# The up-projection of a fused kernel's second block as seven block products in place of eight

## The chip, the cores and the metric

One NeuronCore of a Trainium2 chip runs the whole program. Its engines are TensorE (PE, matmul), whose weight loads are shown apart (PEld), VectorE (DVE), ScalarE (ACT), GpSimd (POOL) and SyncE (SP), which here only issues DMAs. The time is that of one execution on the device in microseconds; lower is better. The comparison is between the kernel before and the changed one.

## The reference

Three stages follow each other. Attention over 2 batches, 8 heads, 768 positions of 64, with a mask that lets a query see only keys of its own hash bucket. A gated block with a spatial projection over the 768 positions (width 512, inner width 1024). And the second block, which the change is about:

```python
mu = np.mean(x, axis=-1, keepdims=True)
var = np.mean((x - mu) ** 2, axis=-1, keepdims=True)
xn = (x - mu) / np.sqrt(var + 1e-06) * g_ln
ch = np.maximum(xn @ w_ch1, 0.0) @ w_ch2
return (x + ch).astype(np.float32)
```

Here x has 2 x 768 = 1536 rows of 512, `w_ch1` is 512 x 2048 and `w_ch2` 2048 x 512. The weights arrive as float64.

## The kernel before, in words

**Precision.** A matmul of the second block is done in three passes of float32r (`PASSES`): each operand is split into a high and a low part, and high x high, high x low and low x high are summed in PSUM (`mm3`). The high part is a copy (`split_hi_v` on ScalarE), the low part a subtraction (`split_lo` on GpSimd, `split_lo_v` on VectorE).

**Weights.** A piece of a weight matrix, 128 x 512 values, is loaded as raw 64-bit words by a DMA that ScalarE issues (`stage_f64`). `words_f64` turns it into two float32 words: one absolute value on ScalarE, then five VectorE operations (clamp, shift and mask, two-operand bit operation, mask, two-operand product). `join_f64` adds the two words on GpSimd, and `split_f64` makes the high part on ScalarE and the low part on GpSimd. In the trace these are `f_w` (the staged words), `f64c_w` (the working tile), `w1t` and `w2t` (the parts). Staging and working tiles have two buffers each (`CB = 2`).

**The second block.** The 2048 inner columns are 16 tiles `f` of 128. The 1536 rows are three chunks `c` of 512 (`TCH`). `up(c, f)` makes one tile of the inner activations transposed, `pc` (128 x 512), with 4 x 3 matmuls of 512 columns; ScalarE writes the relu as high part of `ch`, VectorE the low part, `max(pc, 0) - high`, which reads `pc` in PSUM. `down(c, f)` multiplies `ch`, as the stationary operand, with `w2t[f]` into four accumulators `acc` (one for 128 rows), 4 x 3 matmuls of 512 columns. Not all weights fit, so `runs` visits the chunks in seven runs over ranges of `f`; at the end of a run the accumulators are added to the tiles `ot`, which hold the residual (`residual` loads them from `y_dram`). `second(n)` puts the `up` of one step ahead of the `down` of the step before. The layer norm of a chunk is `ln_stats` (statistics, then `xc`) and `ln_x` (transposes `px_c`, split into `xh`).

**Parts and order.** The program has three parts: the attention with the first gated block of batch 0; part 1, the gated block of batch 1 (`moe1`), with the first steps of the second block as filling (`fill`); and part 2, the rest of the second block. Every engine does all its instructions of a part ahead of those of the next. Inside a part a planner (`Plan`) sets the order: `add` records every operation as a job (up to `RUN` matmuls of one target make one), `run` plays the jobs through with costs of its own, and `issue` writes them out in the order found. An engine other than TensorE may take a job only when TensorE has come within `LOOK` jobs of it (`opened`), and, unless the job is marked `soon`, not more than `EARLY` = 20 us ahead of the latest time (`latest`) at which it is due. All instructions are issued from one line, so every row of the trace has L498; they are told apart by the tiles that they write and read.

## Time and profile before

| | us |
|---|---|
| median of 3 runs (660.79 to 663.34) | 661.33 |
| the profiled execution | 661.69 |
| its span, first to last instruction | 659.6 |

| engine | busy us | share of the span | instructions |
|---|---|---|---|
| PE | 648.2 | 98% | 3386 |
| PEld | 506.7 | 77% | 3386 |
| DVE | 430.1 | 65% | 805 |
| ACT | 302.8 | 46% | 584 |
| POOL | 194.9 | 30% | 185 |

A row of a list of groups reads: line, engine, operation, what it writes <- what it reads, shapes, x count, then busy us, mean ns of one, and the idle time of the engine before them with what ended it. Matmuls are pipelined: the length of one is longer than the distance to the next, and the distance is what it costs.

### The profile page before, as it was taken

What the parts mean: (1) busy time and instruction counts of PE and PEld (TensorE: products, weight loads), DVE (VectorE), ACT (ScalarE), POOL (GpSimd) and SP (SyncE); (2) the same over time, 40 slices, a digit from 0 to 9 for tenths busy, and PEclk for the clock granted to TensorE, in tenths of its full rate; (3) what the DMA queues carried; (4) which work ended last, traced back from release to release, by engine and by line L of the source; (5) the groups of instructions that cost most, each with busy time, mean ns of one, the idle gap of its engine ahead of it and who ended that gap; (6) DMA issues with size and microseconds to landing.
All of it is one profiled execution on the core that took longest, in us unless ns stands there. A gap on an engine that the chain in (4) does not pass through costs nothing.

```text
span 659.6 us, 9420 instructions
## 1 busy us (share of the span) xinstructions
PE 648.2 (98%) x3386; PEld 506.7 (77%) x3386; DVE 430.1 (65%) x805; ACT 302.8 (46%) x584; POOL 194.9 (30%) x185
## 2 busy tenths in 40 slices
PE   7999999999999999999999999999999999999997
PEld 5676667767787787877788888788888888888886
DVE  6879779697886554543897995799862466612122
ACT  6788776876666455433564352533321222311110
POOL 3233424234555311200343331144440134510000
PEclk9999999999999999999999999999999999999999
DMA  6776876668644742606353530733310122200031
GB/s 155 198 196 151 276 168 177 171 145 287 183 114 128 223 104 77 210 16 242 118 210 118 164 93 33 270 97 95 96 34 32 65 64 68 92 1 17 0 112 64
DMA packets 48157, 83.51 MB, mean 127 GB/s; under 512 B 5792, under 2 KB 32112, under 8 KB 47344
## 3 DMA queue, kind: packets, MB, share of 16 engines
q1 hardware_dynamic: 33888, 53.42, 28.6%
q10 hardware_dynamic: 14224, 29.50, 13.7%
q8 instruction: 27, 0.44, 0.3%
q14 instruction: 18, 0.15, 0.1%
HBM read 51.52 MB, written 12.58 MB: 97 GB/s over the span
## 4 chain that ended last, share of the span: by engine, by line
PE 90%; DVE 4%; DMA 2%; ACT 2%; SPq 1%; issue 1%; POOL 0%; DVEq 0%; ACTq 0%
PE pc L498 20%; PE acc L498 20%; PE pv L498 10%; PE po L498 9%; PE sc L498 8%; PE pg L498 8%; PE pt L498 8%; PE py L498 5%; DMA qs<-m 2%; DVE x L498 1%; ACT x L498 1%; PE px_c L498 1%; PE ptr_g L498 1%; SPq L498 1%; DVE f64c_u L498 1%
## 5 line engine op out<-in xcount | busy, mean ns | idle before, releaser
L498 PE MATMUL pc<-xh,w1t 128*128 128x512 f32 x576 | 142.0, 394 | 0.0
L498 PE MATMUL acc<-w2t,ch 128*128 128x512 f32 x576 | 141.8, 393 | 0.0
L498 PEld LDWEIGHTS acc<-w2t,ch 128*128 128x128 f32 x576 | 108.1, 188 | 24.8 <-DVE ot L498 0.2
L498 PEld LDWEIGHTS pc<-xh,w1t 128*128 128x128 f32 x576 | 107.8, 188 | 24.5
L498 ACT ACTIVATE x<-x,nb 128x768 f32<-128x768 f32 x96 | 89.7, 935 | 32.0 <-DVE x L498 30.0
L498 DVE SCALAR_TENSOR_TENSOR ch<-pc,ch 128x512 fp32r<-128x512 f32 x48 | 32.9, 686 | 101.6 <-ACT ch L498 101.6
L498 DVE TENSOR_SCALAR_CACHE_REDUCE x<-sc 128x768 f32<-128x768 f32 x96 | 91.0, 952 | 10.1 <-PE sc L498 3.8
L498 PE MATMUL sc<-ks,qs 128*128 128x512 f32 (+3 forms) x384 | 92.8, 362 | 4.6 <-DMA qs<-m 2.2
L498 ACT ACTIVATE ch<-pc 128x512 fp32r<-128x512 f32 x48 | 28.7, 598 | 130.6 <-PE pc L498 130.1
L498 POOL TENSOR_TENSOR f64c_w<-f_w,f64c_w 128x512 f32<-128x512 f32 x32 | 45.0, 1407 | 133.4 <-DVE f64c_w L498 115.7
L498 PE MATMUL pt<-ident,x 128*128 128x128 f32 x576 | 81.0, 274 | 1.0 <-ACT x L498 0.8
L498 PEld LDWEIGHTS sc<-ks,qs 128*128 128x128 f32 (+1 forms) x384 | 64.1, 190 | 18.9 <-issue 3.6
L498 PEld LDWEIGHTS pt<-ident,x 128*128 128x128 f32 x576 | 66.3, 141 | 13.2 <-issue 4.9
L498 ACT ACTIVATE e<-pt 128x384 f32<-128x384 f32 x120 | 55.3, 485 | 25.3 <-PE pt L498 25.1
L498 PE MATMUL po<-e,vv 128*64 128x384 f32 x384 | 65.5, 490 | 0.0
L498 DVE COPY e<-pt 128x384 f32<-128x384 f32 x72 | 39.6, 552 | 22.3 <-PE pt L498 22.2
L498 PEld LDWEIGHTS po<-e,vv 128*64 128x64 f32 x384 | 26.1, 137 | 31.2 <-issue 29.8
L498 DVE TENSOR_SCALAR f64c_w<-f64c_w 128x512 f32<-128x512 f32 (+1 forms) x64 | 37.3, 587 | 14.1 <-ACT f64c_w L498 13.1
L498 PE MATMUL pg<-vn,w_sp 128*128 128x512 f32 x180 | 43.9, 396 | 0.0
L498 PEld LDWEIGHTS pg<-vn,w_sp 128*128 128x128 f32 x180 | 33.1, 188 | 6.8
L498 ACT ACTIVATE f64c_w<-f_w 128x512 f32<-128x512 f32 x32 | 21.2, 668 | 34.7 <-DMA f_w<-in_w 33.5
L498 PE MATMUL py<-w_out,act_g 128*128 128x512 f32 x144 | 36.0, 396 | 0.0
(131 smaller groups left out, 787.1 us busy)
## 6 DMA issues: line engine op xcount, KB each, us to landing
f_w<-in_w ACTq DMA_DIRECT2D x32, 512.0 KB
ks<-k SPq DMA_DIRECT2D x45, 192.0 KB
qs<-q SPq DMA_DIRECT2D x30, 192.0 KB
wst_sp<-in_w_spT SPq DMA_DIRECT2D x12, 384.0 KB
w_out<-ws_out SPq DMA_DIRECT2D x2, 2048.0 KB
vv<-in_v SPq DMA_DIRECT2D x16, 192.0 KB
ot<-y_dram SPq DMA_DIRECT2D x12, 256.0 KB
qs<-q SPq DMA_DIRECT2D x30, 96.0 KB
```

Of the source, the lines that this page charges most:

```text
L498: getattr(getattr(nc, engine[j.engine]), op)(*map(live, args), **{k: live(x) for k, x in kw.items()})
```

## The change

The rows are cut into four chunks of 384 (`TCH = S // 2`), so that a batch is two chunks. The first four inner tiles (`NA`) are done as before, with matmuls of 384 columns. The other twelve are taken in six pairs `r`. For a pair and a batch the product of a 2 x 2 block matrix of weights (two inner tiles by two halves of the 512 inputs) with a 2 x 2 block matrix of inputs (two halves of the inputs by two chunks) is made from seven block products in place of eight, by sums of weights (`sums` in `w1_pair`, four on VectorE), differences of inputs (`x_forms`) and sums of products (`products`: two copies on ScalarE, five adds on VectorE and two on GpSimd). A pair and a batch are called a unit; there are twelve, in the order (1,2), (0,2), (0,3), (1,3), (1,4), ... The splits of a form into high and low part are made in `parts`. The relu of these tiles is taken from sums held in SBUF (`held`), not from PSUM. Both PSUM banks of the up-projection are taken in turn (`bank`).

The down-projection of a unit (`share`, 2 chunks x 3 row tiles x 2 inner tiles x 3 passes) is issued between the products of the following unit (`late`). Six accumulators are open at once. At the end of a run of units the accumulators are added to their rows, which are read from `y_dram` and written back (`gather_load`, `gather_tile`), the last time into the output. The conversion of the next pair's weights (`convert`) is issued between the products. In the planner `LOOK` is 50 jobs, twice that in part 2, and due times are counted from the first. Conversions in part 2 are marked `soon`.

The chunks' layer norm and the first steps move with the new chunks: in part 1 eight pieces of weights in place of ten, the statistics of three chunks, and the plain steps of chunk 0 and half of chunk 1. The list `fill` of part 1 is left out below, and so are the pools.

```diff
     RUN = 6
-    LOOK = 60
+    LOOK = 50
     EARLY = 20.0
     BULK = 14.0
...
-            i = bisect_left(reached, j.at - self.LOOK)
+            i = bisect_left(reached, j.at - (2 * self.LOOK if j.part > 1 else self.LOOK))
...
-        return late
+        first = min(late.values())
+        return {j: t - first for j, t in late.items()}
...
-    TCH = 512
+    TCH = S // 2
...
-    NA = 5
-    NW = 11
+    NA = 4
+    OB = 2
+    UB = 6
+    NP2 = NF2 // 2
...
+        if f % 2 == 0:
+            pool = m2 if f >= NA and f // 2 % 2 == 0 else m2a
+            w2t[f // 2] = pool.tile([P, 2, 2, DM], F32R, tag="wd", name=f"w2_{f}", bufs=1 if f >= NA and f // 2 % 2 == 0 else 2)
+        to = w2t[f // 2][:, f % 2]
+        if f < NA:
+            load_f64(to[:, 0:1], to[:, 1:2], w2[:, f : f + 1, :], f"w2_{f}")
+        else:
+            tf = join_f64(*words_f64(stage_f64(w2[:, f : f + 1, :], f"w2_{f}"), f"w2_{f}"))
+            hi_a(to[:, 0:1], tf)
+            split_lo(to[:, 1:2], tf, to[:, 0:1])
...
+    def w1_pair(r):
+
+        pool, n = (m2, 7) if r % 2 == 0 else (m2a, 8)
+        two = {}
+
+        def words(a):
+            if a == 0:
+                w1q[r] = pool.tile([P, 2, n, 2, P], F32R, tag="wf", name=f"w1_{r}", bufs=1)
+            f = 2 * r + a
+            nm = f"w1_{f}"
+            st = stage_f64(w1[:, :, f * P : (f + 1) * P], nm)
+            two[a] = join_f64(*words_f64(st, nm))
+            two["st", a] = st
+
+        def sums():
+            s = [two["st", 1][:, m].bitcast(F32).rearrange("p (k m) t -> p k (m t)", k=2) for m in range(4)]
+            two["s"] = s
+            a11, a12, a21, a22 = (two[a][:, 2 * k : 2 * k + 2] for a in range(2) for k in range(2))
+            nc.vector.tensor_tensor(s[0], a21, a22, op=ALU.add)
+            nc.vector.tensor_tensor(s[1], s[0], a11, op=ALU.subtract)
+            nc.vector.tensor_tensor(s[2], a11, a21, op=ALU.subtract)
+            nc.vector.tensor_tensor(s[3], a12, s[1], op=ALU.subtract)
+
+        def parts():
+            q = w1q[r]
+            raw = two[0].rearrange("p (h k) n -> p h k n", h=2)
+            for at, src in (
+                (slice(0, 2), raw),
+                *((3 + m, two["s"][m]) for m in (1, 0, 2)),
+                (2, two[1][:, 2:4]),
+                (6, two["s"][3]),
+            ):
+                hi_a(q[:, 0, at], src)
+                split_lo(q[:, 1, at], src, q[:, 0, at])
+
+        return [lambda: words(0), lambda: words(1), sums, parts]
...
+    def bank(name):
+        turn[0] += 1
+        return ps_c.tile([P, 512], F32, tag=f"p{turn[0] % 2}", name=name, bufs=1)
...
+    def quarter(c, f):
+        chs[c, f] = m2a.tile([P, 2, TCH], F32R, tag="ch", name=f"ch_{c}_{f}", bufs=6)
+        return chs[c, f]
+
+    def relu_split(ch, src):
+        nc.scalar.activation(ch[:, 0], src, AF.Relu)
+        nc.vector.scalar_tensor_tensor(ch[:, 1], src, 0.0, ch[:, 0].bitcast(F32), op0=ALU.max, op1=ALU.subtract)
...
-        pc = ps_c.tile([P, 512], F32, tag="pc", name=f"pc_{c}_{f}")
-        mm3(pc, [(lambda i, k=k: w1t[f][:, i, k, :], lambda j, k=k: xhs[c][:, j, k, :]) for k in range(KFT)])
-        ch = m2a.tile([P, 2, TCH], F32R, tag="ch", name=f"ch_{c}_{f}", bufs=2)
-        nc.scalar.activation(ch[:, 0], pc, AF.Relu)
-        nc.vector.scalar_tensor_tensor(ch[:, 1], pc, 0.0, ch[:, 0].bitcast(F32), op0=ALU.max, op1=ALU.subtract)
-        chs[c, f] = ch
+        pc = bank(f"pc_{c}_{f}")[:, :TCH]
+        w = w1q["A"][:, f]
+        mm3(pc, [(lambda i, k=k: w[:, i, k, :], lambda j, k=k: xhs[c][:, j, k, :]) for k in range(KFT)])
+        relu_split(quarter(c, f), pc)
...
+    def x_forms(b):
+
+        h0, h1 = xhs[2 * b], xhs[2 * b + 1]
+        t = {}
+        for n in (3, 1, 2, 4):
+            for a in range(2):
+                if b:
+                    t[n, a] = m2.tile([P, 2, TCH], F32R, name=f"t{n}{a}_{b}", bufs=1)
+                elif n == 1:
+                    t[n, a] = h1[:, a, 0:2]
+                else:
+                    t[n, a] = m2a.tile([P, 2, TCH], F32R, tag="xc", name=f"t{n}{a}_{b}", bufs=6)
+        if not b:
+            for c, h in enumerate((h0, h1)):
+                rxs[c] = m2.tile([P, KFT, TCH], F32, tag=f"rx{c}", name=f"rx_{c}", bufs=1)
+                for k in (0, 2):
+                    nc.gpsimd.tensor_tensor(
+                        rxs[c][:, k : k + 2],
+                        h[:, 0, k : k + 2].bitcast(F32),
+                        h[:, 1, k : k + 2].bitcast(F32),
+                        op=ALU.add,
+                    )
+        r11, r21, r12, r22 = (rxs[2 * b + c][:, k : k + 2] for c in range(2) for k in (0, 2))
+        for n, to, x, y in ((1, r11, r12, r11), (3, r12, r22, r12), (2, r22, r22, r11), (4, r21, r21, r22)):
+            nc.vector.tensor_tensor(to, x, y, op=ALU.subtract)
+            hi_a(t[n, 0], to)
+            (split_lo_v if n % 2 else split_lo)(t[n, 1], to, t[n, 0])
+        forms[b] = {
+            "B11": lambda j, k: h0[:, j, k],
+            "B21": lambda j, k: h0[:, j, 2 + k],
+            "B22": lambda j, k: h1[:, j, 2 + k],
+            **{f"T{n}": lambda j, k, n=n: t[n, j][:, k] for n in (1, 2, 3, 4)},
+        }
...
+    def products(b, r):
+
+        f0, f1, c0, c1 = 2 * r, 2 * r + 1, 2 * b, 2 * b + 1
+        q, rhs = w1q[r], forms[b]
+        nm = f"{b}_{r}"
+
+        def product(n, a, x):
+            ps = bank(f"p{n}_{nm}")[:, :TCH]
+            for m, (k, (i, j)) in enumerate((k, ij) for k in range(2) for ij in PASSES):
+                nc.tensor.matmul(ps, q[:, i, a, k], rhs[x](j, k), start=(m == 0), stop=(m == 5))
+            return ps
+
+        def held(n):
+            return m2.tile([P, TCH], F32, tag="u", name=f"u{n}_{nm}", bufs=UB)
+
+        def plus(to, x, y, e=nc.vector):
+            e.tensor_tensor(to, x, y, op=ALU.add)
+
+        u, c = held(1), held(2)
+        nc.scalar.activation(u, product(1, 0, "B11"), AF.Copy)
+        yield
+        plus(c, product(2, 1, "B21"), u)
+        relu_split(quarter(c0, f0), c)
+        yield
+        plus(u, product(6, 4, "T2"), u)
+        yield
+        w, v = held(5), held(7)
+        nc.scalar.activation(w, product(5, 3, "T1"), AF.Copy)
+        yield
+        plus(v, product(7, 5, "T3"), u)
+        plus(u, u, w, nc.gpsimd)
+        plus(w, w, v, nc.gpsimd)
+        yield
+        x = held(4)
+        plus(x, product(4, 2, "T4"), v)
+        relu_split(quarter(c0, f1), x)
+        yield
+        relu_split(quarter(c1, f1), w)
+        plus(u, product(3, 6, "B22"), u)
+        relu_split(quarter(c1, f0), u)
+        yield
...
+    def share(c, t, fs, start, stop):
+
         if start:
-            accs[c] = [ps_y.tile([P, 512], F32, tag="py", name=f"acc_{c}_{f}_{t}") for t in range(TPC)]
-        for t in range(TPC):
+            at = c % 2 * TPC + t
+            pool, tag = (ps_n, "m") if c > 1 and at > 3 or c < 2 and plan.part == 2 and at > 3 else (ps_y, "py")
+            accs[c, t] = pool.tile([P, 512], F32, tag=tag, name=f"acc_{c}_{fs[0]}_{t}")
+        for f in fs:
+            ch = chs[c, f]
             for n, (i, j) in enumerate(PASSES):
                 nc.tensor.matmul(
-                    accs[c][t],
+                    accs[c, t],
                     ch[:, i, t * P : (t + 1) * P],
-                    w2t[f][:, j, 0, :],
-                    start=(start and n == 0),
-                    stop=(stop and n == 2),
+                    w2t[f // 2][:, f % 2, j],
+                    start=(start and f == fs[0] and n == 0),
+                    stop=(stop and f == fs[-1] and n == 2),
...
+    def gather_load(c, last=False):
+        if last and c > 1:
+            if c == 3:
+                ots["last"] = m2a.tile([P, 2, TPC, DM], F32, tag="xh0", name="ots_last", bufs=1)
+            ots[c] = ots["last"][:, c - 2]
+        else:
+            ots[c] = m2.tile([P, TPC, DM], F32, tag=f"rx{c % 2}", name=f"ots_{c}", bufs=1)
+        nc.sync.dma_start(out=ots[c], in_=y_dram[c * TPC : (c + 1) * TPC].rearrange("t p d -> p t d"))
+
+    def gather_tile(c, t, last=False, end=False):
+        n = c * TPC + t
+        ot = ots[c][:, t]
+        to = outv[n] if last else y_dram[n]
+        for a, cols in enumerate([slice(k * DM // 2, (k + 1) * DM // 2) for k in range(2)] if end else [slice(0, DM)]):
+            nc.vector.tensor_tensor(ot[:, cols], accs[c, t][:, cols], ot[:, cols], op=ALU.add)
+            (nc.scalar if a else nc.sync).dma_start(out=to[:, cols], in_=ot[:, cols])
...
-    runs = [(0, 0, NA), (1, 0, NA), (2, 0, NW), (1, NA, NW), (0, NA, NF2), (1, NW, NF2), (2, NW, NF2)]
-    cf = [(c, f, f == at, f == to - 1) for c, at, to in runs for f in range(at, to)]
-    todo = []
-
-    def second(n):
-        if n < len(cf):
-            up(*cf[n][:2])
-        if 1 <= n <= len(cf):
-            down(*cf[n - 1])
+    ps_c = Pool(plan, "ps_c", 1, part=1, after=(ps_s, ps_b), space=PSUM, reuse_waits="tile")
+    ps_y = Pool(plan, "ps_y", 4, part=1, after=(ps_b,), space=PSUM, reuse_waits="tile")
+
+    def plain(c, f):
+
+        if f < NA:
+            up(c, f)
+        if f:
+            down(c, f - 1, f == 1, f == NA and c < 2)
...
+    todo = []
+
+    def convert(r):
+        todo.extend(w1_pair(r))
+        todo.extend([lambda: w2_piece(2 * r), lambda: w2_piece(2 * r + 1)])
+
+    def next_todo():
+        plan.soon = True
+        if todo:
+            todo.pop(0)()
+        plan.soon = False
+
+    convert(NA // 2)
+    for f in range(NA + 1):
+        plain(2, f)
+        next_todo()
+        if f == 0:
+            for t in range(TPC):
+                ln_x(3, t)
+    for f in range(NA + 1):
+        plain(3, f)
+        if f < NA:
+            next_todo()
+        if f == 0:
+            x_forms(1)
+    while todo:
+        next_todo()
+    units = []
+    for r in range(NA // 2, NP2):
+        units.extend([(1, r), (0, r)] if r % 2 == 0 else [(0, r), (1, r)])
+    runs = []
+    for b, r in units:
+        if runs and runs[-1][0] == b:
+            runs[-1][1].append(r)
+        else:
+            runs.append((b, [r]))
+    late = []
+    for n, (b, rs_of) in enumerate(runs):
+        for m, r in enumerate(rs_of):
+            u = units.index((b, r))
+            if n == 0:
+                convert(r + 1)
+            elif m == len(rs_of) - 1 and r + 1 < NP2:
+                convert(r + 1)
+            if u == 0:
+                x_forms(0)
+            for _ in products(b, r):
+                if late:
+                    late.pop(0)()
+                next_todo()
+            while late:
+                late.pop(0)()
+            first, end = n > 0 and m == 0, m == len(rs_of) - 1
+            last = r == NP2 - 1
+
+            final = last and n == len(runs) - 1
+
+            def piece(c, t, fs, r=r, first=first, end=end, last=last, final=final):
+                share(c, t, fs, first and fs[0] == 2 * r, end and fs[-1] == 2 * r + 1)
+                if end and fs[-1] == 2 * r + 1:
+                    if t == 0:
+                        gather_load(c, last)
+                    gather_tile(c, t, last, final and c % 2 == 0 and t == TPC - 1)
+
+            both = (2 * r, 2 * r + 1)
+            for c, fs in ((2 * b, both[:1]), (2 * b + 1, both), (2 * b, both[1:])) if final else ((2 * b + 1, both), (2 * b, both)):
+                late.extend(lambda c=c, t=t, fs=fs, p=piece: p(c, t, fs) for t in range(TPC))
...
```

## Rows read from the trace of the kernel before

**Rows 1.** Page: busy us (share of the span) x instructions; granted clock in 40 slices.
```profile
PE 648.2 (98%) x3386; PEld 506.7 (77%) x3386; DVE 430.1 (65%) x805; ACT 302.8 (46%) x584; POOL 194.9 (30%) x185
...
PEclk9999999999999999999999999999999999999999
```

**Rows 2.** Waits of PE, longest first: us in total, times, longest.
```profile
PE sc L498 <- DMA qs<-m: 2.2, 2, 1.6
PE sc L498 <- DVE x L498: 1.6, 2, 0.9
...
```

**Rows 3.** Timeline of PE in the second block: start us, length us, what, count.
```profile
597.48 2.96 PE L498 MATMUL pc<-xh,w1t 128*128 128x512 f32 x12
...
603.03 2.96 PE L498 MATMUL pc<-xh,w1t 128*128 128x512 f32 x12
```

**Rows 4.** Groups by form, whole span: matmuls of `pc`, weight loads of `acc`.
```profile
L498 PE MATMUL pc<-xh,w1t 128*128 128x512 f32 x576 | 142.0, 394 | 0.0
...
L498 PEld LDWEIGHTS acc<-w2t,ch 128*128 128x128 f32 x576 | 108.1, 188 | 24.8 <-DVE ot L498 0.2
```

**Rows 5.** Stretches: us, PE, PEld, DVE, ACT, POOL busy (x), clock, DMA share, GB/s.
```profile
340.00:360.00 20.00, 20.00 (x90) 16.34 (x89) 18.31 (x39) 9.20 (x15) 9.57 (x8) 1.00 0.39 125
...
440.00:460.00 20.00, 20.00 (x88) 16.29 (x87) 18.69 (x24) 6.21 (x10) 9.56 (x7) 1.00 0.33 97
...
480.00:500.00 20.00, 20.00 (x89) 16.30 (x88) 10.27 (x13) 4.17 (x7) 6.51 (x5) 1.00 0.10 28
```

**Rows 6.** Timeline of PE at one score tile: 512, 256, 256 columns, then transposes.
```profile
121.68 0.64 PE L498 MATMUL sc<-ks,qs 76*128 76x512 f32 x3
122.16 0.60 PE L498 MATMUL pt<-ident,x 128*128 128x128 f32 x4
```

**Rows 7.** Groups by form, whole span: prices of other engines' operations.
```profile
L498 POOL TENSOR_TENSOR w1t<-f64c_w,w1t 128x512 fp32r<-128x512 f32 x16 | 21.0, 1315 | 10.9 <-ACT w1t L498 8.9 <-issue 1.8 <-POOL r_c L498 0.2
...
L498 ACT ACTIVATE e<-pt 128x384 f32<-128x384 f32 x120 | 55.3, 485 | 25.3 <-PE pt L498 25.1
...
L498 DVE COPY e<-pt 128x384 f32<-128x384 f32 x72 | 39.6, 552 | 22.3 <-PE pt L498 22.2
...
L498 POOL TENSOR_TENSOR w_sp<-wst_sp,w_sp 128x768 fp32r<-128x768 f32 x6 | 11.1, 1853 | 39.2 <-PE pg L498 37.7 <-issue 1.6
...
L498 DVE TENSOR_TENSOR w_sp_early<-wst_sp,w_sp_early 128x768 fp32r<-128x768 f32 x2 | 1.9, 948 | 0.0
...
L498 DVE TENSOR_TENSOR ot<-acc,ot 128x256 f32<-128x256 f32 x2 | 0.8, 420 | 0.0
```

**Rows 8.** Tile `f64c_w`, 425 to 470 us: ns shortest/median/longest, first and last start.
```profile
L498 DVE TENSOR_SCALAR f64c_w<-f64c_w x16: 409/428/1555, 426.1 to 468.9; 128x512 f32<-128x512 f32 x8, 128x512 uint32<-128x512 uint32 x8
L498 DVE SCALAR_TENSOR_TENSOR f64c_w<-f_w,f64c_w x8: 676/681/693, 425.5 to 466.5; 128x512 f32<-128x512 uint32 x8
...
L498 DVE SCALAR_TENSOR_TENSOR f_w<-f_w,f64c_w x8: 675/693/1837, 428.5 to 469.3; 128x512 uint32<-128x512 uint32 x8
L498 DVE TENSOR_SCALAR f64c_w<-f_w x7: 426/1401/1414, 429.2 to 466.0; 128x512 uint32<-128x512 uint32 x7
```

**Rows 9.** Timeline of all engines from 431.9 us: GpSimd's join and VectorE beside it.
```profile
431.92 1.31 POOL L498 TENSOR_TENSOR f64c_w<-f_w,f64c_w 128x512 f32<-128x512 f32 x1 [1.56 <-DVE f64c_w L498]
432.16 1.82 DVE L498 TENSOR_SCALAR f64c_w<-f64c_w 128x512 f32<-128x512 f32 x2 [0.32 <-ACT f64c_w L498]
```

**Rows 10.** Tiles `ch`, `w_sp` and `k`: ns shortest/median/longest, first and last start.
```profile
L498 DVE SCALAR_TENSOR_TENSOR ch<-pc,ch x48: 655/691/695, 341.6 to 651.0; 128x512 fp32r<-128x512 f32 x48
...
L498 DVE TENSOR_TENSOR w_sp<-wst_sp,w_sp x4: 948/1590/2032, 355.6 to 392.6; 128x768 fp32r<-128x768 f32 x4
...
L498 POOL TENSOR_TENSOR k<-k x14: 1006/1013/1728, 24.4 to 222.3; 128x384 fp32r<-128x384 f32 x14
```

**Rows 11.** Timeline of ACT where part 2 begins: first weight loads, first word.
```profile
412.83 0.94 ACTq L498 DMA_DIRECT2D f_w<-in_w  x2
...
417.06 0.66 ACT L498 ACTIVATE f64c_w<-f_w 128x512 f32<-128x512 f32 x1 [0.79 <-DMA f_w<-in_w]
```

110 lines of the change are left out of this document (56 added, 54 removed).

## The prediction, made before the changed kernel was timed

> **What bounds the kernel now.** I read the page first: TensorE is busy 98% of the span at full clock, and no other engine comes near [rows 1]. A busy PE need not be a PE at its peak, so the waits come next: the two longest that the trace finds for TensorE, 2.2 and 1.6 us, belong to the scores `sc` of the attention, and nothing of the second block is in the list [rows 2]. The timeline of PE in the second block shows what its time is made of: twelve matmuls `pc` (up) and twelve `acc` (down) follow each other, and from one `pc` run to the next it takes 603.03 - 597.48 = 5.55 us, so 0.2312 us for each matmul of 512 columns [rows 3]. That is the price of the second block: 576 + 576 matmuls [rows 4] at 0.2312 = 266 of the 659.6 us. Fewer columns through TensorE is a gain one for one, as long as the other engines keep feeding it. How near these are to not doing so the table of stretches shows [rows 5]: VectorE is busy 18.3 and 18.7 of 20 us at 340 and 440, with GpSimd at 9.6 beside it, and TensorE never stops there; from 480 VectorE is down to 10, and the DMA engines to a tenth.
>
> **The change, part by part.**
>
> *Up-projection, removed and added.* Before: 16 inner tiles x 3 chunks x 12 matmuls = 576 of 512 columns, 576 x 0.2312 = 133.2 us. After: four tiles stay plain, 4 x 4 chunks x 12 = 192 matmuls of 384 columns; the other twelve are six pairs, each with 2 batches x 7 products x 6 matmuls, 504 of 384 columns. Together 696. The trace has no float32r matmul of 384 columns. The timeline of one score tile gives 256: from the start of the 76-row matmul of 512 columns to the next transpose it takes 122.16 - 121.68 = 0.48 us for one of 512 and two of 256 columns, so (0.48 - 0.231) / 2 = 0.1245 us each [rows 6]. Between that and 0.2312 lies 0.178; in proportion to the columns it would be 0.173. I take 0.175: 696 x 0.175 = 121.8 us, a gain of 11.4 us (9.3 at 0.178, 12.8 at 0.173).
>
> *Down-projection and transposes.* 16 tiles x 12 token tiles x 3 = 576 matmuls of 512 columns as before, and 48 transposes `px_c` as before: 0.
>
> *What the seven products ask of the others.* Prices: a VectorE operation of 384 columns 0.55 us (copies `e`), of 512 0.68, of 256 0.42, of 768 0.95; ScalarE at 384 0.485; GpSimd's two-operand operation 1.32 at 512, 1.01 at 384 (shortest and median), 1.85 at 768 [rows 7, 8, 10]. VectorE: 12 units x 5 adds x 0.55 = 33.0; six pairs x 4 weight sums x 0.42 = 10.1; input differences and their splits 12 x 0.95 = 11.4; the accumulators are now gathered 48 instead of 29 times, 19 x 0.68 = 12.9; the relu splits 64 x 0.55 against 48 x 0.687 = +2.2. Sum +70 us. GpSimd: low parts of the weight forms, 1792 columns a pair where two tiles had 1024, 6 x 1.5 x 1.32 = 11.9; 24 adds x 1.01 = 24.2; input sums and splits 8 x 1.85 = 14.8. Sum +51 us. ScalarE: 24 copies x 0.485, and by estimates between these prices some 18 us more for small casts and copies: +30 us onto 303, no bound. All of this hides if TensorE's order leaves it time. If nothing covered it, VectorE's +70 alone would cost more than the gain six times over, so the cover is the question.
>
> *The cover, per weight pair.* Two units take TensorE 2 x (42 x 0.175 + 36 x 0.2312) = 31.3 us. In that time VectorE has four float64 pieces at 0.42 + 0.69 + 0.42 + 0.68 + 0.42 = 2.63 us when nothing hinders them (shortest times [rows 8]), 10.5 us; four sums, 1.7; 18 operations of the units, 9.9; six gathers, 4.1: 26.2 us. GpSimd has four joins, two low parts of w2, 1792 columns of w1 forms and four adds: (4 + 2 + 3.5) x 1.32 + 4 x 1.01 = 16.6 us. Both fit 31.3 by themselves. But they hinder each other: in the dense conversions the clamp and the masks take up to 1.4 to 1.56 us instead of 0.42 [rows 8], and the timeline shows why: GpSimd runs from 431.92 to 433.23, and VectorE's two operations from 432.16, 0.85 us when unhindered, take 1.82, to 433.98 [rows 9]. The relu split `ch` reads PSUM and one SBUF tile and is never stretched (655 to 695 ns), while the subtraction `w_sp`, which reads two SBUF tiles, goes from 948 to 2032 [rows 10]. After the change 48 of 64 relu splits read two SBUF tiles, and so do the sums.
>
> The Trainium skill (SBUF — State Buffer, "Who interferes with whom") says the same as a rule: a VectorE instruction with two SBUF inputs and a GpSimd instruction that reads SBUF exclude each other, and the loser waits for the whole instruction. By that rule the port would pace the change, and the sum would be that of rival 2 below, 676 in place of 654. The stretched operations of rows 8 and 10 agree with it, and so does the unstretched `ch`.
>
> What speaks against its full price: the stretch at 340 already runs at 18.31 + 9.57 = 27.9 us of both engines in 20, TensorE unhindered [rows 5], where the pair asks for (26.2 + 16.6) x 20 / 31.3 = 27.3. So for the pairs I take a wait of 0 (ends: 0, and 3.6 us a pair, below).
>
> *Where a wait is likeliest.* The differences of batch 0 (`x_forms(0)`) fall between the plain tiles and the second unit: 6 x 0.95 on VectorE and 6 x 1.85 on GpSimd, 16.8 us, beside a pair that fills both. Ahead of it conversions start late: in part 2 ScalarE issues weight loads only behind the last copy of part 1; today that is at 412.83, and the first word is worked on at 417.06 [rows 11]. TensorE then has eight plain tiles at 12 x 0.175 + 9 x 0.2312 = 4.18, 6.3 us of chunk 1 and 24 transposes (four in 0.60 us [rows 6], so under 3.6) before the first unit: some 42 us. I let half of the 16.8 run ahead there, and half of the rest hide: 4 us of TensorE waiting (ends: 0 and 17). Queued behind it on VectorE, and on SP's queue by the buffers that they share, are the gathers that free the accumulators, which TensorE needs only a unit (15.7 us) later.
>
> *DMAs.* Each gather of a run now reads and writes back three tiles of 256 KB through SP, 42 tiles each way. Of the DMA engines' time 0.33 and less is used here from 440 on [rows 5], and a load is issued well before its unit ends: 0 (up to 3 at the first run, whose buffers `x_forms(0)` holds).
>
> *Start and end of part 2.* Chunk 2's normalised input now has 6.3 us of work in front (one tile and a down pass of chunk 1) where it had a whole run; three tiles, each two copies on ScalarE of at most 0.66 (a word's copy of as many columns [rows 11]), 4 us, fit: 0 (up to 2). The end is the same chain, last accumulator, one add in halves, store: 0.
>
> **Sum.** 659.6 - 11.4 + 4.0 = 652.2 us of span. The profiled execution took 661.69, 2.1 over its span, and is 0.36 over the median of 661.33: 652.2 + 2.1 - 0.4 = 653.9, say 654.
>
> **Rivals.**
>
> 1. *All hidden.* The planner puts the differences into the plain tiles and TensorE never waits, as it never does today: 650. For it: today's list of waits and the stretch at 340 [rows 2, 5]. Against: VectorE has 5 us free a pair where GpSimd works 16.6.
>
> 2. *The shared port sets the pace, slower.* Place: the five pairs converted beside units. A pair's operations that hinder each other are GpSimd's 16.6 us and VectorE's pieces, sums and eight relu splits, 10.5 + 1.7 + 8 x 0.55 = 16.6: 33.2 us in 31.3. In the dense stretch GpSimd's two operations and the unhindered five of VectorE fill 2 x 1.32 + 2.63 = 5.27 of each 5.55 us [rows 3, 7, 8], 95%; at the same density a pair needs 34.9, 3.6 more than TensorE's 31.3, five times 18, and half of `x_forms(0)` another 8: 661.3 - 11.4 + 26 = 676. It decides against the change from 2.3 us a pair (5 x 2.3 = 11.4). Against: today's stretch shows how full it was, not that it could not go faster, for TensorE set its rhythm.
>
> 3. *Waits of about the gain.* Half of rival 2, 13 us: 663.
>
> 4. *Weight loads set the pace of short matmuls.* A LDWEIGHTS lasts 188 ns [rows 4]; if they could not overlap, 696 x 0.188 = 130.8 and the gain is 2.4: 659, 663 with the waits. Against: the matmuls of 256 columns, each with a load of its own, at 0.1245 [rows 6].
>
> **How the numbers follow.** Forecast with a few us of waits (651.5 to 658): 0.44. All hidden (under 651.5): 0.19. Rival 3: 0.13, rival 4: 0.04, both within half a per cent. Rival 2: 0.20. Half a per cent, 3.3 us, is about what a measurement tells from no change: faster (below 658.0) 0.63, same 0.17, slower (above 664.6) 0.20. The range takes in the lower end of the matmul price with no waits (661.3 - 12.8 = 648.5) and reaches to 668, part way into rival 2: 648.5 to 668.
>
> **What the profile after would show.** Matmuls of 384 columns following at 0.175 us, 696 of them; if 0.188, rival 4. TensorE waits of some us in front of the first units of batch 0, behind the input differences: my step. Waits spread over every pair, released by VectorE or GpSimd, with relu splits stretched past 0.55 us: rival 2. No waits at all: rival 1. VectorE busy near 500, GpSimd near 246. The prediction is wrong if the stretches between 460 and 615 show TensorE idle by more than 2 us a pair.

## The result and the profile after

| | median us (lowest to highest) | ratio to before, 95% interval |
|---|---|---|
| before | 662.42 (660.79 to 663.64) | |
| after | 672.13 (668.69 to 674.98) | 1.0149 [1.0112, 1.0186] |

The change made the kernel slower; the prediction said 654. The profiled execution of after took 672.35, its span is 670.6 us. All its instructions have L499.

The page, its busy line, as in [rows 1]:

```profile
PE 645.4 (96%) x3506; PEld 522.7 (78%) x3506; DVE 512.4 (76%) x942; ACT 334.5 (50%) x662; POOL 265.7 (40%) x242
```

TensorE has 120 instructions more, is busy 2.8 us less, and its share fell from 98 to 96%: the span grew by idle time. The waits of PE, as in [rows 2] (us in total, times, longest):

```profile
PE p L499 <- DVE u L499: 4.5, 5, 1.6
PE pc L499 <- DVE ch L499: 3.5, 1, 3.5
...
PE px_c L499 <- ACT xc L499: 1.7, 1, 1.7
...
PE p L499 <- ACT u L499: 1.3, 2, 0.9
PE pc L499 <- ACT w_a L499: 1.3, 1, 1.3
PE pc L499 <- POOL w_a L499: 0.8, 1, 0.8
```

All six are of the second block, which had none before. The table of stretches says where, as in [rows 5]:

```profile
340.00:360.00 20.00, 17.94 (x81) 14.38 (x79) 19.93 (x47) 9.37 (x16) 8.27 (x7) 1.00 0.61 220
360.00:380.00 20.00, 20.00 (x97) 17.69 (x98) 15.20 (x28) 9.45 (x16) 8.29 (x6) 0.92 0.16 52
...
440.00:460.00 20.00, 16.15 (x73) 14.05 (x73) 20.00 (x18) 6.71 (x13) 17.87 (x11) 0.91 0.08 26
460.00:480.00 20.00, 19.31 (x100) 17.14 (x98) 16.67 (x19) 8.54 (x14) 12.27 (x9) 1.00 0.17 53
480.00:500.00 20.00, 18.64 (x90) 16.08 (x91) 20.00 (x33) 7.45 (x16) 11.99 (x11) 1.00 0.58 170
500.00:520.00 20.00, 20.00 (x99) 17.56 (x97) 18.04 (x29) 6.55 (x12) 9.59 (x7) 1.00 0.57 199
520.00:540.00 20.00, 18.28 (x92) 16.10 (x91) 19.93 (x32) 7.65 (x16) 11.71 (x11) 1.00 0.53 165
540.00:560.00 20.00, 19.59 (x97) 17.22 (x96) 17.79 (x30) 6.50 (x13) 13.13 (x11) 1.00 0.45 152
560.00:580.00 20.00, 18.94 (x95) 16.84 (x95) 17.60 (x28) 7.58 (x16) 11.70 (x11) 1.00 0.62 211
580.00:600.00 20.00, 19.09 (x96) 16.76 (x95) 18.92 (x33) 8.23 (x17) 11.43 (x11) 1.00 0.48 157
600.00:620.00 20.00, 20.00 (x100) 17.69 (x99) 18.26 (x31) 7.09 (x14) 10.67 (x8) 1.00 0.38 120
```

The deepest hole is 440 to 460, in the plain tiles, ahead of the first unit (its first `p` starts at 465.81). VectorE is busy 20 of 20 us there with 18 instructions and GpSimd 17.87 with 11; at 340 before, 39 and 8 took 18.31 and 9.57. The timeline of PE in that stretch (start, length, what, count, and the wait ahead):

```profile
455.15 2.02 PE L499 MATMUL pc<-xh,w_a 128*128 128x384 f32 x6 [3.46 <-DVE ch L499]
456.96 3.14 PE L499 MATMUL acc<-w,ch 128*128 128x512 f32 x9
459.95 2.25 PE L499 MATMUL pc<-xh,w_a 128*128 128x384 f32 x12
462.03 2.20 PE L499 MATMUL acc<-w,ch 128*128 128x512 f32 x9
464.07 1.21 PE L499 MATMUL pc<-xh,w_a 128*128 128x384 f32 x6
```

The matmul of 384 columns is as predicted: twelve in 462.03 - 459.95 = 2.08 us, 0.173 each. The wait of 3.46 us is for the relu split `ch`, and VectorE's timeline shows what held it up, with GpSimd's beside it:

```profile
446.95 2.60 DVE L499 TENSOR_TENSOR rx<-rx,rx 128x768 f32<-128x768 f32 x1
...
449.81 2.61 DVE L499 TENSOR_TENSOR t<-rx,t 128x768 fp32r<-128x768 f32 x1
452.35 2.28 DVE L499 SCALAR_TENSOR_TENSOR f_w<-f_w,f64c_w 128x512 uint32<-128x512 uint32 x1
454.55 0.54 DVE L499 SCALAR_TENSOR_TENSOR ch<-pc,ch 128x384 fp32r<-128x384 f32 x1
```

```profile
446.71 2.03 POOL L499 TENSOR_TENSOR t<-rx,t 128x768 fp32r<-128x768 f32 x1
449.69 1.92 POOL L499 TENSOR_TENSOR rx<-xh 128x768 f32<-128x768 f32 x1 [0.95 <-POOL t L499]
451.57 2.51 POOL L499 TENSOR_TENSOR t<-rx,t 128x768 fp32r<-128x768 f32 x1
454.05 6.21 POOL L499 TENSOR_TENSOR rx<-xh 128x768 f32<-128x768 f32 x3
```

The three VectorE operations shown ahead of `ch` read two SBUF tiles each and take 2.60 + 2.61 + 2.28 = 7.5 us where their unhindered prices are 0.95, 0.95 and 0.68 [rows 7, 8]. Each lies beside a 768-column operation of `x_forms` on GpSimd and ends under a microsecond after it: the first at 449.55, GpSimd's at 448.74. The tile `ch` tells the two kinds apart (ns shortest/median/longest):

```profile
L499 DVE SCALAR_TENSOR_TENSOR ch<-u,ch x48: 541/548/1661, 472.8 to 659.3; 128x384 fp32r<-128x384 f32 x48
...
L499 DVE SCALAR_TENSOR_TENSOR ch<-pc,ch x16: 518/550/558, 341.4 to 465.8; 128x384 fp32r<-128x384 f32 x16
```

The split from PSUM is never stretched, the one from SBUF up to 1661 ns. That is the Trainium skill's rule that the prediction quotes, two SBUF inputs against GpSimd's reads (SBUF — State Buffer, "Who interferes with whom"), and the trace agrees with it. The 60 adds `u` that free the banks read a product in PSUM, and they are never stretched either; what can be late is what stands ahead of them in VectorE's queue:

```profile
L499 DVE TENSOR_TENSOR u<-p,u x60: 539/545/559, 469.2 to 657.0; 128x384 f32<-128x384 f32 x60
```

**Time lost by stage.** To compare kernels I sum, from the records, the distance from each PE instruction's start to the next one's beyond what is usual for its shape (0.231 us for 512 columns, 0.175 for 384, 0.122 for 256, 0.109 for 128; excesses over 0.06 us only, so slow-clock matmuls count too; the attention's `po` and `pm` are left out). The stages end with the last `po`, the last `py`, the first `p`, the last `p`. Such a loss is larger than the idle time in the list of waits, in the units 9.4 against 4.5 + 1.3 us: the list counts only from the recorded end of the matmul ahead, and slow matmuls behind a wait count here too.

| | attention | part 1 | plain tiles | units |
|---|---|---|---|---|
| before | 22.7 | 1.2 | 0.4, both together | |
| after | 24.4 | 7.3 | 6.4 | 9.4 |

1.7 + 6.1 + 15.4 = 23.2 us lost more, less the 11.4 saved, is 11.8; the spans differ by 11.0.

### The profile page after: what moved, and what is told of

Same layout as the page of the kernel before. It is cut to its first block, busy times and chain, and to the rows that moved or that the text cites. A ratio compares the mean times of both kernels' runs of the same rounds, so it can differ in the third digit from the quotient of the medians.

```text
span 670.6 us, 10059 instructions
## 1 busy us (share of the span) xinstructions
PE 645.4 (96%) x3506; PEld 522.7 (78%) x3506; DVE 512.4 (76%) x942; ACT 334.5 (50%) x662; POOL 265.7 (40%) x242
## 5 line engine op out<-in xcount | busy, mean ns | idle before, releaser
L499 PE MATMUL acc<-w,ch 128*128 128x512 f32 x576 | 143.4, 395 | 0.4 <-DVE ch L499 0.4
L499 PEld LDWEIGHTS acc<-w,ch 128*128 128x128 f32 x576 | 108.0, 189 | 21.1 <-DVE ch L499 1.5
L499 ACT ACTIVATE x<-x,nb 128x768 f32<-128x768 f32 x96 | 89.7, 935 | 27.2 <-DVE x L499 26.8
L499 DVE TENSOR_SCALAR_CACHE_REDUCE x<-sc 128x768 f32<-128x768 f32 x96 | 90.8, 952 | 14.0 <-PE sc L499 10.7
L499 PE MATMUL sc<-ks,qs 128*128 128x512 f32 (+3 forms) x384 | 93.8, 364 | 4.4 <-issue 2.2
L499 PE MATMUL pt<-ident,x 128*128 128x128 f32 x576 | 82.2, 277 | 0.8 <-DVE e L499 0.2
L499 POOL TENSOR_TENSOR f64c_w<-f_w,f64c_w 128x512 f32<-128x512 f32 x32 | 46.7, 1460 | 81.3 <-DVE f64c_w L499 65.8
L499 PEld LDWEIGHTS pt<-ident,x 128*128 128x128 f32 x576 | 67.4, 142 | 14.5 <-issue 4.0
L499 PEld LDWEIGHTS sc<-ks,qs 128*128 128x128 f32 (+1 forms) x384 | 63.4, 192 | 16.9 <-issue 3.3
L499 ACT ACTIVATE e<-pt 128x384 f32<-128x384 f32 x120 | 55.6, 485 | 26.5 <-PE pt L499 26.2
L499 PE MATMUL po<-e,vv 128*64 128x384 f32 x384 | 65.5, 490 | 0.0
L499 DVE COPY e<-pt 128x384 f32<-128x384 f32 x72 | 39.6, 552 | 23.7 <-PE pt L499 22.8
L499 PE MATMUL p<-xh,w 128*128 128x384 f32 x252 | 50.4, 341 | 4.8 <-DVE u L499 4.5
L499 PEld LDWEIGHTS p<-xh,w 128*128 128x128 f32 x252 | 44.3, 188 | 9.8 <-DVE u L499 7.7
L499 PEld LDWEIGHTS po<-e,vv 128*64 128x64 f32 x384 | 26.1, 137 | 31.2 <-issue 29.7
L499 PE MATMUL p<-t,w 128*128 128x384 f32 x252 | 49.0, 338 | 1.3 <-ACT u L499 1.3
L499 PEld LDWEIGHTS p<-t,w 128*128 128x128 f32 x252 | 44.2, 188 | 3.8 <-ACT u L499 2.3
L499 ACT ACTIVATE ch<-u 128x384 fp32r<-128x384 f32 x48 | 24.6, 524 | 43.5 <-DVE u L499 40.5
L499 POOL TENSOR_TENSOR w<-f64c_w,w 128x512 fp32r<-128x512 f32 (+1 forms) x28 | 36.7, 1310 | 23.7 <-ACT w L499 16.3
L499 DVE TENSOR_SCALAR f64c_w<-f64c_w 128x512 f32<-128x512 f32 (+1 forms) x64 | 39.9, 627 | 8.0 <-ACT f64c_w L499 7.8
L499 PE MATMUL pc<-xh,w_a 128*128 128x384 f32 x192 | 39.7, 354 | 5.5 <-DVE ch L499 3.5
L499 PE MATMUL pg<-vn,w_sp 128*128 128x512 f32 x180 | 43.9, 396 | 0.0
```

Source lines behind the costliest of these rows:

```text
L499: getattr(getattr(nc, engine[j.engine]), op)(*map(live, args), **{k: live(x) for k, x in kw.items()})
```

## The experiments

Each edit is to the changed kernel unless it says before. The last columns are the time lost by stage, as above.

Two cautions go with the table. The planner orders all instructions anew for each edit, also in stages that the edit leaves alone ("told in part 2", whose edit is to part 2 only, differs from after in the order of TensorE's work from 13.6 us on). So a few us in a stage can come from the new order and not from what the edit took away. And the losses are those of one profiled execution: for "quarters on VectorE" it took 674.65 us, the longest of ten, for "told, quarters on VectorE" 662.45.

| kernel | median us (range) | ratio, 95% interval | attention | part 1 | plain | units |
|---|---|---|---|---|---|---|
| look-ahead 60 | 676.36 (674.99 to 677.92) | 1.0210 [1.0186, 1.0233] | 25.6 | 5.5 | 8.4 | 11.3 |
| before, look-ahead 50 | 663.35 (661.92 to 667.88) | 1.0024 [1.0003, 1.0045] | 24.6 | 2.3 | 1.2 | |
| before, fill packed | 682.23 (680.57 to 682.61) | 1.0305 [1.0284, 1.0325] | 36.4 | 8.5 | 0.3 | |
| statistics later | 675.95 (670.68 to 676.96) | 1.0195 [1.0151, 1.0240] | 24.5 | 10.7 | 5.1 | 11.6 |
| eight products | 666.53 (665.99 to 669.52) | 1.0079 [1.0049, 1.0108] | 21.7 | 4.8 | 3.3, both | |
| adds in PSUM | 674.20 (671.68 to 676.00) | 1.0174 [1.0144, 1.0203] | 22.3 | 5.8 | 5.0 | 16.5 |
| no low parts of forms | 669.37 (667.72 to 671.58) | 1.0104 [1.0070, 1.0137] | 27.0 | 6.8 | 5.8 | 6.1 |
| no run sums | 668.73 (667.41 to 670.26) | 1.0103 [1.0075, 1.0132] | 25.4 | 6.8 | 7.4 | 4.4 |
| both left out | 665.01 (662.79 to 667.53) | 1.0055 [1.0030, 1.0079] | 21.8 | 6.7 | 1.3 | 10.1 |
| light quarters | 660.99 (658.72 to 663.25) | 0.9985 [0.9965, 1.0004] | 21.8 | 4.3 | 5.9 | 3.5 |
| quarters on VectorE | 669.97 (665.47 to 674.65) | 1.0099 [1.0066, 1.0132] | 26.4 | 6.6 | 4.6 | 12.5 |
| planner told, all parts | 676.13 (674.51 to 679.79) | 1.0219 [1.0179, 1.0259] | 26.5 | 12.8 | 0.4 | 11.2 |
| told in part 2 | 666.59 (665.72 to 669.24) | 1.0083 [1.0057, 1.0109] | 23.6 | 6.2 | 0.4 | 10.9 |
| told, light quarters | 653.25 (652.22 to 653.82) | 0.9850 [0.9814, 0.9886] | 21.3 | 4.7 | 0.4 | 2.7 |
| told, quarters on VectorE | 659.56 (657.61 to 662.81) | 0.9965 [0.9939, 0.9990] | 24.4 | 6.5 | 0.4 | 5.3 |
| told, every relief | 658.25 (656.63 to 660.12) | 0.9926 [0.9901, 0.9952] | 23.1 | 3.9 | 1.3 | 7.3 |
| the same, no loads | 654.00 (653.67 to 657.05) | 0.9885 [0.9862, 0.9908] | 22.0 | 5.4 | 1.3 | 0.1 |
| told, VectorE, loads in three | 657.04 (655.31 to 661.76) | 0.9934 [0.9911, 0.9957] | 22.4 | 6.1 | 0.4 | 4.2 |

Only six of the eighteen medians lie in a range that their expectation gave: "before, look-ahead 50", "both left out" (by its time, not by the loss that it named), "told in part 2", "told, quarters on VectorE" and the last two.

**Look-ahead 60**, and **before, look-ahead 50** with due times counted from the first, as after has them.

```diff
-            i = bisect_left(reached, j.at - (2 * self.LOOK if j.part > 1 else self.LOOK))
+            i = bisect_left(reached, j.at - (100 if j.part > 1 else 60))
```

> The changed kernel, but the planner's look-ahead in the attention and in part 1 is 60 jobs again (100 in part 2 stays). Theory W (the shorter window makes the 2 us lost in the attention and the 7 us of TensorE waits in part 1): about 664 us instead of 672, the waits for the layer norm of chunk 0 and for the first weight parts gone. Theory P (the port shared by VectorE and GpSimd is the cause everywhere): 670 to 674, part 1 as before.

> The kernel before with only the two planner edits of the change: look-ahead 50 jobs instead of 60 and due times counted from the first. Theory W: slower than before by some 5 to 9 us, 667 to 671. Theory P: 661 to 664, since no port work is added.

Look-ahead 60 doesn't take the loss away, and the two settings slow the kernel before by 0.24%, with 1.1 us more lost in part 1, where after lost 6.1 more: the planner's settings are at most a small part of the cause.

**Before, fill packed.** The kernel before, with the pieces and steps of part 1 at steps as close as the changed kernel has them.

```diff
-        (10, lambda: w1_piece(2)),
-        (12, lambda: second(1)),
-        (13, lambda: w2_piece(2)),
-        (14, lambda: w1_piece(3)),
-        (15, lambda: second(2)),
-        (16, lambda: w2_piece(3)),
+        (8, lambda: w1_piece(2)),
+        (9, lambda: second(1)),
+        (10, lambda: w2_piece(2)),
+        (10, lambda: w1_piece(3)),
+        (11, lambda: second(2)),
+        (12, lambda: w2_piece(3)),
```

> The kernel before, with the first four tiles' weights and steps packed into the same places of part 1 as in the changed kernel (weights of tiles 2 and 3 two to four steps earlier). If the packing makes the loss ahead of part 2, part 1 loses 4 us or more instead of 1.2 and the time is 664 to 667; if not, 661 to 663.

20 us slower with no product changed. Its PE timeline in part 1 waits for weights, as after does:

```profile
357.54 1.20 PE L498 MATMUL pc<-xh,w1t 128*128 128x512 f32 x4 [0.96 <-POOL w1t L498]
...
379.88 3.57 PE L498 MATMUL acc<-w2t,ch 128*128 128x512 f32 x8 [1.11 <-POOL w2t L498]
```

8.5 - 1.2 = 7.3 us are lost there, about what after lost (6.1). The other 13.7 lie in the attention, which the edit doesn't touch but which is ordered anew; its waits of PE now begin with loads:

```profile
PE sc L498 <- DMA qs<-q: 6.5, 2, 4.2
PE sc L498 <- DMA ks<-k: 2.3, 1, 2.3
```

**Statistics later.** In part 1 the statistics of chunk 1 at step 11.

```diff
-        *((6, lambda t=t: ln_stats(1, t)) for t in range(TPC)),
+        *((11, lambda t=t: ln_stats(1, t)) for t in range(TPC)),
```

> The changed kernel, but the statistics of chunk 1 stand five steps later in the list of part 1, so that they don't press on VectorE when chunk 0 and the first weights are made. If their early place makes the 7 us lost in part 1: 666 to 669. If VectorE is too full there in any order: 670 to 674.

Part 1 got worse, 10.7. A fill as widely spaced as before's wasn't tried.

**Eight products.** Units with eight plain products; no sums or differences; chunks of 384, fill and run sums as after. Four tiles in place of seven products make a unit, so two pieces of the down-projection, not one, follow each.

```diff
-        u, c = held(1), held(2)
-        nc.scalar.activation(u, product(1, 0, "B11"), AF.Copy)
...
+        for c in (2 * b, 2 * b + 1):
+            for a in range(2):
+                ps = bank(f"pc_{c}_{2 * r + a}")[:, :TCH]
...
+                relu_split(quarter(c, 2 * r + a), ps)
```

> The changed kernel with the eight plain block products in the units: chunks of 384, the order of units and runs, the gathers and the conversion stay, but no weight sums, no input differences and no sums of products. TensorE has 72 matmuls of 384 columns more, 72 x 0.174 = 12.5 us. If the sums cause the waits of part 2 (16 us), they go: 672 - 16 + 12.5 = 668 to 670, with the 9 us that are lost ahead of part 2 still there; if those go too, 660 to 662. If the new order and the gathers cause the waits: 680 or more.

Part 2 loses 3.3 us in place of 15.8, with 12.5 us more work on TensorE to hide the rest behind: the sums and differences bring the waits there. Part 1 still loses 4.8 of its 7.3, so most of that loss is the moved work's.

**Adds in PSUM.** Products 2, 4 and 3 are added to in their bank, and three of four relu splits read PSUM.

```diff
-        plus(c, product(2, 1, "B21"), u)
+        c = product(2, 1, "B21")
+        plus(c, c, u)
```

> The changed kernel, but three of the four sums of a unit that a relu is taken from are added in place in the PSUM bank of their last product, so that 36 of the 48 relu splits read one SBUF tile instead of two; VectorE and GpSimd do as many operations as before. Theory P: these splits fall from 0.80 to about 0.55 us, and of the 9 us that TensorE loses among the units some 4 to 6 come back: 666 to 668. Theory D (VectorE simply has too much work, with or without the port): 671 to 673.

Those 36 splits take 549 ns on average, never stretched, yet the units lose 16.5. The two banks are held longer, and PE waits for them:

```profile
PE p L499 <- DVE ch L499: 6.9, 7, 2.6
```

**No low parts of forms, no run sums, both left out.** What they leave out stands in their expectations.

```diff
-                split_lo(q[:, 1, at], src, q[:, 0, at])
+                hi_a(q[:, 1, at], src)
...
-            nc.vector.tensor_tensor(ot[:, cols], accs[c, t][:, cols], ot[:, cols], op=ALU.add)
+            nc.scalar.activation(ot[:, cols], accs[c, t][:, cols], AF.Copy)
```

> The changed kernel, but the low parts of the w1 forms are not subtracted on GpSimd: ScalarE copies the form itself in their place, so that the low part is left out of the computation. It takes 36 operations and 37 us of GpSimd time away and not one of VectorE. Theory P (GpSimd and VectorE exclude each other): the 9 us lost among the units fall to 3 or less and part of the 6 us in the plain tiles goes, 662 to 666. Theory D (VectorE has too much work of its own): 670 to 674.

> The changed kernel, but at the end of a run ScalarE copies the accumulators out in place of the 42 VectorE adds, so that the sums with the earlier runs and with the residual are left out. It takes 27 us of VectorE time away, of operations that read one SBUF tile, and none of GpSimd. Theory D: 662 to 666. Theory P: the port is as full as before, 1 to 3 us, 669 to 671.

> The changed kernel with both leave-outs at once: w1's low parts copied by ScalarE (37 us of GpSimd less) and the accumulators copied out by ScalarE (27 us of VectorE less); low parts and run sums are left out of the computation. If the waits among the units come from VectorE's queue, filled by its own work and by the port together, the 9 us lost there fall to under 2 (they fell to 6 and to 4 with one leave-out each): 664 to 667, with the losses of the plain tiles and of part 1 as they were. If something else holds TensorE there: 668 or more.

Each alone is worth about 3 us. Plain tiles and units together lose 15.8 us in after, 11.9 and 11.8 with one leave-out, and 11.4 with both: the second brings nothing there, and with both the units lose 10.1 again. So the loss doesn't follow the amount of work. About half of the 7 us that both bring lies in the attention and part 1.

**Light quarters, and quarters on VectorE.** The differences' GpSimd work goes: to copies on ScalarE (left out in part), or whole to VectorE.

```diff
-                    nc.gpsimd.tensor_tensor(
...
+                    hi_a(rxs[c][:, k : k + 2], h[:, 0, k : k + 2].bitcast(F32))
...
-            (split_lo_v if n % 2 else split_lo)(t[n, 1], to, t[n, 0])
+            split_lo_v(t[n, 1], to, t[n, 0]) if n % 2 else hi_a(t[n, 1], to)
```

```diff
-                    nc.gpsimd.tensor_tensor(
+                    nc.vector.tensor_tensor(
...
-            (split_lo_v if n % 2 else split_lo)(t[n, 1], to, t[n, 0])
+            split_lo_v(t[n, 1], to, t[n, 0])
```

> The changed kernel, but the input forms need no GpSimd: the sums for batch 0 are copies of the high part and the low parts of two of the four differences are copies of the form, both by ScalarE, so that low parts are left out. It takes the 8 GpSimd operations of 768 columns away, 17 us, most of them between 446 and 460 us. Theory P: VectorE's differences fall from 2.6 us to 0.95 and the 6 us lost in the plain tiles fall under 2: 666 to 668. Theory D: they stay, 671 to 674.

> The changed kernel with the input forms made by VectorE alone: sums for batch 0 and all four low parts, 8 operations of 768 columns moved from GpSimd. VectorE has 7.6 us more work than in the changed kernel, GpSimd 17 us less. Theory P: the time falls, as it did when the 8 were left out (661), but less, since VectorE gets the work: 663 to 667. Theory D: VectorE's work rises, so the time does, 674 or more.

Eight GpSimd operations away bring 11 us: 5.9 in the units, 5.6 in attention and part 1, which the edit doesn't touch but which are ordered anew. The plain tiles, where the operations lay, still lose 5.9. A relu split waits there as before, now behind three differences, two of them stretched by low parts of weights:

```profile
438.95 1.50 DVE L499 TENSOR_TENSOR t<-rx,t 128x768 fp32r<-128x768 f32 x1
440.38 2.03 DVE L499 TENSOR_TENSOR rx<-rx,rx 128x768 f32<-128x768 f32 x1
442.33 0.94 DVE L499 TENSOR_TENSOR t<-rx,t 128x768 fp32r<-128x768 f32 x1
443.20 0.54 DVE L499 SCALAR_TENSOR_TENSOR ch<-pc,ch 128x384 fp32r<-128x384 f32 x1
```

```profile
443.80 3.19 PE L499 MATMUL acc<-w,ch 128*128 128x512 f32 x7 [2.72 <-DVE ch L499]
```

The three take 4.5 us there, 2.9 unhindered, and TensorE waits 2.7. So the collisions lengthen the wait, and the place of the differences in VectorE's queue makes it. With the same work on VectorE the gain is 2 us, and the intervals of the two ratios overlap: it may be none.

**Planner told, all parts, and in part 2 only.** The planner counted conversions and relu splits without a PSUM operand as hindered by GpSimd already; now it counts the two-operand sums and differences too. The operations stay the same, only their order changes. The first edit has no `job.part > 1`; the second is shown.

```diff
-            job.shared = not psum and op in ("tensor_scalar", "scalar_tensor_tensor")
+            job.shared = not psum and (op in ("tensor_scalar", "scalar_tensor_tensor") or op == "tensor_tensor" and job.part > 1)
```

> The changed kernel, but the planner is told that a two-operand VectorE operation on SBUF tiles alone waits for GpSimd; only the order of the instructions changes. Theory O (the order was found by a planner that did not see these collisions): 663 to 668, most of the waits in the plain tiles (6 us) and among the units gone. Theory P as a plain limit of work: 670 to 674, the same exclusive work in another order.

> The changed kernel, with the planner told of the collisions of two-operand VectorE operations in part 2 alone. With this told everywhere the plain tiles lost 0.4 us instead of 6.4, but part 1 lost 12.8 instead of 7.3. If that was the order: part 1 as in the changed kernel (7), the plain tiles under 1, the units 9 to 11: 666 to 669. If the attention and part 1 are planned anew by chance: 670 to 676.

The loss of the plain tiles is gone, 6.4 to 0.4, by order alone. Its stretch at 440:

```profile
440.00:460.00 20.00, 20.00 (x104) 18.34 (x104) 17.54 (x17) 7.14 (x14) 19.01 (x11) 1.00 0.15 48
```

GpSimd is fuller than in after, and TensorE never stops. The table bears it out: in all seven versions with a told planner the plain tiles lose 0.4 to 1.3 us, without it 4.6 to 8.4 in eight of nine (the ninth, both left out, 1.3). The units gain nothing from it alone, 10.9. Told in all parts, part 1 is ordered worse (12.8).

**Told, light quarters; told, quarters on VectorE; told, every relief.** These are the edits above together.

> The planner told, and the 8 GpSimd operations of the input forms replaced by ScalarE copies, so that low parts are left out. Theory P and O: 655 to 658. If the order that is told costs what it saves: 660 to 662 as without it.

> The same with the planner told of the collisions of part 2. Theory P and O together: losses of 1 in the plain tiles and 3 to 5 among the units, 657 to 662, the best of the versions that compute everything. Theory D: 668 or more.

> All leave-outs at once with the planner told: input forms without GpSimd, w1's low parts and the run sums copied by ScalarE; GpSimd loses some 54 us and VectorE 27 in part 2. If load and collisions of these two engines are what took the gain, TensorE loses under 1 us in part 2 and the time is 661.4 - 11.4 + 6 (part 1 and the attention, as they were) = 655 to 657. If more than 3 us are lost in part 2, something else holds TensorE.

The first is at 653 us. The second computes everything and is 0.35% under the kernel before, with an interval that ends 0.1% under it. The third has the least work and yet loses more in the units than the first. Its timeline of ACT there shows a weight load issued at 456.39 whose first word is worked on at 464.98, 8.6 us later (4.2 in [rows 11]); two gather loads of 768 KB went out at 455.62:

```profile
456.39 0.39 ACTq L499 DMA_DIRECT2D f_w<-in_w  x1
...
464.98 0.66 ACT L499 ACTIVATE f64c_w<-f_w 128x512 f32<-128x512 f32 x1 [3.35 <-DMA f_w<-in_w]
```

VectorE stands behind it with the clamp of that piece, and the add `u` that frees a bank is queued after the clamp; then PE:

```profile
465.67 0.89 DVE L499 TENSOR_SCALAR f64c_w<-f64c_w 128x512 f32<-128x512 f32 x2 [2.93 <-ACT f64c_w L499]
466.47 0.55 DVE L499 TENSOR_TENSOR u<-p,u 128x384 f32<-128x384 f32 x1
```

```profile
467.08 2.97 PE L499 MATMUL p<-xh,w 128*128 128x384 f32 x12 [1.84 <-DVE u L499]
```

This wait, with matmuls at half rate behind it, costs 3.7 of the 7.3 us, and one at 562 behind another late word 0.65. Most of the other 3 us stands behind stretched operations: ahead of 536 two relu splits, 2.14 us where two unhindered take 1.0, hold the add `u` that PE waits for.

```profile
533.61 2.14 DVE L499 SCALAR_TENSOR_TENSOR ch<-u,ch 128x384 fp32r<-128x384 f32 x2
```

```profile
536.26 1.31 PE L499 MATMUL p<-xh,w 128*128 128x384 f32 x6 [0.56 <-DVE u L499]
```

**The same, no loads; and told, quarters on VectorE, loads in three.**

```diff
-        nc.sync.dma_start(out=ots[c], in_=y_dram[c * TPC : (c + 1) * TPC].rearrange("t p d -> p t d"))
```

```diff
-        nc.sync.dma_start(out=ots[c], in_=y_dram[c * TPC : (c + 1) * TPC].rearrange("t p d -> p t d"))
+        for t in range(TPC):
+            nc.sync.dma_start(out=ots[c][:, t], in_=y_dram[c * TPC + t])
```

> As the kernel with every relief at once (658.25 us, ratio 0.9926; it leaves out the low parts in the forms of w1 and of the quarters, the sums of the two quarters of batch 0 and the run sums), and the loads that bring the earlier runs back for the run sums are left out too. Theory M (weight loads behind these loads land late): the 7.3 us that TensorE loses in the units fall under 3, time 652 to 655. Rival D (the planned order of VectorE and GpSimd alone): 7 us stay, time 657 to 660.

> As the kernel that tells the planner of the collisions in part 2 and makes the sums and low parts of the quarters on VectorE alone (659.56 us, ratio 0.9965), but the run sums that a gather reads back come as three loads of 256 KB instead of one of 768 KB. It computes everything. Theory M (weight loads issued right behind a gather's loads land late, and the forms behind them wait): the 5.3 us that TensorE loses in the units fall to about 3, time 656 to 659. Rival D (what is lost in the units is the work of VectorE and GpSimd in the planned order, whatever the loads do): 5 us stay, time 659 to 661.

Without the gather loads the units lose 0.1 us, 7.2 less, and the median falls by 4.2. Late words were some 4 of the 7.2; the rest can be the new order's, which the edit brings too. All that PE waits for from 420 us on is:

```profile
PE pc L499 <- DVE ch L499: 0.6, 1, 0.6
```

Loads cut in three move the complete kernel from 5.3 to 4.2 us lost, with intervals of the ratio that overlap, so a gain from this isn't shown; it is the fastest version that computes everything, 0.66% under before.

## Why the prediction was wrong, step by step

The sum has 4.0 us of waiting. What was lost beyond the kernel before is 23.2 us: 9.4 in the units, 6.0 in the plain tiles, 6.1 in part 1 and 1.7 in the attention.

- **Up-projection, 11.4 us: right.** 0.173 us for each matmul of 384 columns, and the sum of the stages closes with it to 0.8 us. Rival 4 is out.
- **"So for the pairs I take a wait of 0": failed.** The units lose 9.4 us, 7.0 of them after 482. The step compared busy times by stretch; the stretch at 340 was as full, but only two relu splits fell into it (341.60 and 354.95). Now 60 adds free TensorE's two banks, in one queue with 48 relu splits and with conversions and sums that stretch or whose words come late. With eight plain products the same conversions cost part 2 only 3.3.
- **`x_forms(0)`, 4 us beside the first units: mis-placed, and too small.** Between the plain tiles and the second unit, where the 4 us were put, two waits cost 2.4 us (they end at 477.5 and 481.4). The differences of batch 1, on which no wait was put, and six of GpSimd's eight 768-column operations, among them the four sums of batch 0 that were to run ahead for nothing, lie in the plain tiles, before the first unit, and 6.4 us are lost there. The stretching is that of [rows 8 to 10]; what it cost came from the order, which "told in part 2" shows, not from the amount.
- **Part 1: no cost put on it, failed.** The prediction costed the moved pieces in part 2 alone. The fill of part 1 lost 6.1 us more than before; the kernel before loses 7.3 more when its fill alone is packed. No term stood for a new order of the attention either (1.7).
- **Gathers' DMAs, 0: failed where it could be seen.** The DMA share is 0.53 to 0.58 in the units from 480 to 540, against 0.10 at 480 before [rows 5]. In "told, every relief" late words make some 4 of the 7.3 us that the units lose. In the changed kernel late words stand ahead of two waits of PE, 2.0 us of the 9.4, and at both the clamp behind the word is stretched as well: of the larger one the clamp takes 1.28 us in place of 0.42, beside a join of GpSimd:

```profile
575.50 1.28 DVE L499 TENSOR_SCALAR f64c_w<-f64c_w 128x512 f32<-128x512 f32 x1
```

- **Rival 2, 676, was nearest in time, and its collisions are real, but its place and law were not right.** It came near by luck: its 26 us are 18 in the five pairs and 8 for `x_forms(0)`, where 23.2 were lost, 13.8 of them outside the units. It priced a port full over five pairs. The longest wait is ahead of the pairs; between 460 and 620 PE's busy time falls short in six stretches of eight, by 6.2 us in all, 1.2 a pair, under the 2 that the prediction named. And "told, light quarters" runs the same five pairs with 2.7 us lost in the units.
- **The stretched operations of [rows 8], read by the rule: in part wrong.** The prediction says that the stretched operations agree with a rule on two SBUF inputs. The two-operand ones do; the clamp and the masks, stretched to as much as 1.56 us, read one SBUF tile, and the rule as it stands there doesn't cover them.
- **VectorE near 500, GpSimd near 246:** 512.4 and 265.7; most of the excess is stretching.

What stays open: why the attention loses between 21.3 and 27.0 us in these versions of the changed kernel, by the order planned; how much of the units' 9.4 is collision and how much the order of the queue; and which part of the moved work makes the loss of part 1. Whether the 11.4 us can be had in full isn't shown: 653 us with light quarters and a told planner is 1.5% under before but leaves work out, and the best that computes everything is 0.66% under.

## What to carry to other kernels

Work taken from the bounding engine pays one for one only if what replaces it is on time: price not the helpers' busy sum but the queue in front of each operation that frees a buffer of the bounding engine. When a change moves prefetch work into an earlier stage, cost that stage too. Where an order is planned from prices, give the planner the collisions before judging the change.
